# Attention, ELU block and routed experts on one core: three instruction orders around PSUM banks, and another way to spread the routing's maximum

## The chip, the cores and the metric

The kernel runs on one core of one Trainium2 chip. The metric is the device time of one execution in microseconds (us), taken as the median of several runs. The core has TensorE (PE in the profile, PEld for its weight loads), VectorE (DVE), ScalarE (ACT), GpSimd (POOL) and SyncE (SP, which here only issues DMAs). Matmuls write into the eight banks of PSUM. VectorE and ScalarE read the results from there.

## The reference, cut to what matters

Three stages follow one another. The middle one is the ELU block, the last one the routed experts:

```python
x = attention(q, k, v)                        # window of 64 keys, 4 x 8 heads, 2304 tokens in all
x = elu(x @ w_in) @ w_out                     # 512 -> 2048 -> 512
logits = x @ w_gate                           # 2304 x 8
logits = logits - logits.max()                # one maximum over the whole matrix
P = np.exp(logits)
for _ in range(8):
    P /= P.sum(1, keepdims=True) + 1e-09
    P /= P.sum(0, keepdims=True) + 1e-09
    P *= N / E
for e in range(8):
    out += P[:, e:e+1] * (np.maximum(x @ w1[e], 0.0) @ w2[e])
```

## The kernel before, in words

The order of every engine's instructions is the order in which the Python code emits them. The whole kernel stands in one manually scheduled block, and each engine, and each engine's DMA queue, works through its own list in that order. Products keep fp32 accuracy: an operand is split into a high and a low part, and three products (high by high, high by low, low by high) are added up in PSUM. So a block of 384 columns is six matmuls for a 256-row operand, and so on.

The attention comes first, then the ELU block. When the last blocks of the ELU block are done, the logits are formed, and the routing's parts (`sink_parts`, lines 625 to 697) are emitted one by one between the steps of the first experts. Part `p0` (line 629) takes the maximum of the logits along the free axis with VectorE, line 631, so that each of 128 partitions has its own maximum `mx`. Part `p1` (line 639) turns that column into a row by a product with the identity (line 641) and reduces the row to one negated number `nb` on one partition (line 643). Part `p2` (line 646) spreads that number over 128 partitions by a product with a row of ones (line 648), copies it out of PSUM (line 650) and takes the exponential on ScalarE (line 651). Then `rows` (lines 656 to 665) and `cols` (lines 667 to 674) do the eight normalizations. Each `cols` adds up the partitions by a product with ones (`csum`, line 669). Between them run the first experts in a simple form, `e_in` (lines 965 to 979, tile `p`, low part at line 260) and `e_out` (lines 981 to 999, tile `ac`, summed at line 1009). At the same time the weights for later are prepared: GpSimd makes sums of weight blocks (line 784), ScalarE their high parts (line 799) and VectorE their low parts (line 804).

The rest of the experts (from 639 us on) runs as a fast matrix scheme with seven block products in place of eight. Its loop, from line 1687 on, has a counter `s`. Seven values of `s` make one period. A period has one token group `g` of three and one quarter of an expert's hidden width. In each step there are two calls of `l1` (first product, tiles `la` and `lb`, two PSUM banks each, line 1205) and, eight steps later, one call of `l2` (second product, tiles `oa` and `ob`, line 1374 for group 0 and line 1287 in `l2_flip` for the others). `pairs` (line 1028) says which two of the seven products (`pi`) a step forms, and `out_order` (line 1033) the order of the second products. An accumulated first product is read out between its parts: `keep` copies `la` to SBUF on ScalarE (line 1225, tiles `a`, `u`, `v`), and later parts are added onto the same bank. VectorE adds such a copy to `lb` (lines 1219 and 1245), which frees that bank. The scaled form for groups 1 and 2 multiplies by the routing weights at line 1215. The high parts of the hidden values are made by ScalarE (`hid`, line 1178) and the low parts by VectorE or GpSimd (`hid_low`, lines 1183 and 1187). These wait in the list `after`, of which each call of `l1` takes up to two, and are emitted behind the call's own instructions. Some weights come raw and are split on the way: high by ScalarE (line 1113), low by GpSimd (line 1115), emitted by `w_part`.

For group 0 a second product is weighted and added to the output sum by three VectorE instructions (line 1392). In the last period of the group these write the tile `fo`, which SyncE's queue sends out (line 1397). For groups 1 and 2 the output sum stands transposed, and is added at line 1304. At the very end most of it is transposed by VectorE (line 1330) and sent by 16 DMAs, half of them issued by ScalarE's queue (line 1336). The last four 128-column blocks are transposed by TensorE in `out_unit` (line 1316) into the two `lb` banks (tile `ot`), copied out by ScalarE (line 1321; for the last block, `c == 3`, by VectorE, line 1319) and sent by SyncE's queue (line 1323).

Of the kernel before, what the change touches and what calls it, by code (L numbers as in the profile page):

```python
# [11 lines left out]
AF = mybir.ActivationFunctionType  # L12
ALU = mybir.AluOpType
AX = mybir.AxisListType
# [4 lines left out]
def kernel(  # L19
# [14 lines left out]
    nc = tc.nc  # L34
# [3 lines left out]
    E, _, FF = w1.shape  # L38
    P = 128
# [24 lines left out]
    mask = const.tile([P, P], F32, name="mask")  # L64
# [18 lines left out]
    ident = const.tile([P, P], F32, name="ident")  # L83
    ones = const.tile([P, P], F32, name="ones")
    Lg = const.tile([P, NTT, E], F32, name="Lg")
    Pr = const.tile([P, NTT, E], F32, name="Pr")
# [24 lines left out]
    def ps_sm(name):  # L111
        return ps.tile([P, 512], F32, tag="sm", bufs=1, name=name)
# [510 lines left out]
    sk = {}  # L623

    def sink_parts():
        def small(shape, nm):
            return const.tile(shape, F32, name=nm)

        def p0():
            mx = small([P, 1], "mx")  # L630
            nc.vector.tensor_reduce(mx, Lg, axis=AX.XY, op=ALU.max)
            sk["mx"] = mx
            t = work.tile([P, TB], F32, tag="m", bufs=2, name="Pe")
            Pe = t[:, :(NTT + 1) * (E + 1)].rearrange("p (t e) -> p t e", e=E + 1)
            nc.gpsimd.memset(Pe[:, :, E:], 1e-9)
            nc.gpsimd.memset(Pe[:, NTT], 1e-9 / P)
            sk["Pe"], sk["Pw"] = Pe, Pe[:, :NTT, :E]

        def p1():
            t = ps_sm("mxT")  # L640
            nc.tensor.matmul(t[0:1, :P], sk["mx"], ident, start=True, stop=True)
            nb = small([1, 1], "nb")
            nc.vector.tensor_reduce(nb, t[0:1, :P], axis=AX.X, op=ALU.max, negate=True)
            sk["nb"] = nb

        def p2():
            t = ps_sm("nbB")
            nc.tensor.matmul(t[:, 0:1], ones[0:1, :], sk["nb"], start=True, stop=True)
            nm = small([P, 1], "nm")
            nc.vector.tensor_copy(nm, t[:, 0:1])  # L650
            nc.scalar.activation(sk["Pw"], Lg, AF.Exp, bias=nm)
            sk["rs"] = small([P, NTT], "rs")
            sk["cs"] = small([P, E], "cs")
            sk["rc"] = small([P, E], "rc")

        def rows():
            rs, cs = sk["rs"], sk["cs"]
            nc.vector.tensor_reduce(rs, sk["Pe"][:, :NTT], axis=AX.X, op=ALU.add)
            nc.vector.reciprocal(rs, rs)
            nc.vector.tensor_tensor(  # L660
                out=sk["Pw"], in0=sk["Pw"], in1=rs.unsqueeze(2).to_broadcast([P, NTT, E]), op=ALU.mult
            )
            nc.vector.tensor_reduce(
                cs, sk["Pe"][:, :, :E].rearrange("p t e -> p e t"), axis=AX.X, op=ALU.add
            )

        def cols(to=None):
            t = ps_sm("csum")
            nc.tensor.matmul(t[:, :E], ones, sk["cs"], start=True, stop=True)
            rc = sk["rc"]  # L670
            nc.vector.reciprocal(rc, t[:, :E])
            nc.vector.scalar_tensor_tensor(
                sk["Pw"] if to is None else to, sk["Pw"], float(NT) / E, rc.unsqueeze(1).to_broadcast([P, NTT, E]),
                op0=ALU.mult, op1=ALU.mult,
            )

        def first():
            p2()
            rows()

        def mid():
            cols()
            rows()

        def flip():
            f = Pr.rearrange("p t e -> p (t e)")
            n = NTT * E - P
            t = ps_sm("prT")
            nc.tensor.transpose(t[:, 0:P], f[:, 0:P], ident)
            nc.tensor.transpose(t[:n, P:2 * P], f[:, P:], ident)  # L690
            st = work.tile([P, TB], F32, tag="m", bufs=2, name="prT")
            nc.scalar.activation(st[:, 0:P], t[:, 0:P], AF.Copy)
            nc.scalar.activation(st[:n, P:2 * P], t[:n, P:2 * P], AF.Copy)
            nc.sync.dma_start(out=prd[0:P], in_=st[:, 0:P])
            nc.sync.dma_start(out=prd[P:P + n], in_=st[:n, P:2 * P])

        return [p0, p1, first] + [mid] * 7 + [lambda: cols(Pr), flip]


# [470 lines left out]

    chains = {}
    H = {}
    after, late = [], []

    def hid(key, slot, src, relu):
        h = P2["hp"].tile([P, 2, TH], R32, tag=f"h{slot}", bufs=3, name=f"h{slot}")
# [15 lines left out]
    def l1(k, n, p, pi):  # L1192
# [20 lines left out]
        def scaled(t, i):  # L1213
            if g:
                nc.vector.tensor_tensor(out=t, in0=t, in1=pb[g, e][:, i], op=ALU.mult)  # L1215
# [18 lines left out]
        if pi == 1:  # L1234
            keep("a")
        elif pi == 2:
            add("c11", "a")
            put(0, "c11", True)
        elif pi == 6:
            keep("u")  # L1240
        elif pi == 5:
            keep("v")
            c = d["C"][:, :TH]
            t = tmp("c", 5, "c22")
            nc.vector.tensor_tensor(out=t, in0=c, in1=d["v"], op=ALU.add)  # L1245
            scaled(t, 1)
            d["c22"] = t
            put(2, "c22", True)
        elif pi == 3:
            d["r21"] = tmp("s", 6, "r21")  # L1250
            if g:
                nc.vector.scalar_tensor_tensor(
                    d["r21"], o, 0.0, pb[g, e][:, 1], op0=ALU.max, op1=ALU.mult
                )
            else:
                nc.scalar.activation(d["r21"], o, AF.Relu)  # L1256
            ssum("s3", "c11", "r21", ALU.subtract)
            ssum("s1", "c22", "r21", ALU.add)
            ssum("s2", "c11", "s1", ALU.subtract)
            put(5, "s3", False)  # L1260
            put(4, "s2", False)
            put(3, "s1", False)
        elif pi == 4:
            def rest():
                add("c21", "u")
                ssum("s4", "c21", "s2", ALU.add)
                put(1, "c21", True)
                put(6, "s4", False)

            late.append(rest)  # L1270
            del chains[key]
# [40 lines left out]
    def out_unit(g, acT, i, c):  # L1312
        o = P2["ps2"].tile([P, 512], F32, tag="lb", bufs=2, name="ot")
        for t in range(TH // P):
            a = i * TH + t * P
            nc.tensor.transpose(o[:, t * P:(t + 1) * P], acT[:, c, a:a + P], ident)
        st = tmp("s", 6, "ost")
        if c == 3:
            nc.vector.tensor_copy(st, o[:, :TH])
        else:  # L1320
            nc.scalar.activation(st, o[:, :TH], AF.Copy)
        t0 = (2 * g + i) * TH
        nc.sync.dma_start(
            out=out[t0:t0 + TH, c * P:(c + 1) * P].rearrange("(t p) d -> p t d", p=P),
            in_=st.rearrange("p (t d) -> p t d", d=P),
        )
# [16 lines left out]
    ot = {}  # L1343
    banks = ["oa", "ob"]

    def l2(k, x):
        g, e, pp = periods[k]
        pi = out_order[x]
        if x == 0:
# [31 lines left out]
                    )  # L1381
        if done:
            fo = P2["fin"].tile([P, 3, HB2], F32, tag=f"o{i}{j}", name="fo")
        for c in range(3):
            tt = 3 * i + c
            pe = Pr[:, g * 6 + tt, e:e + 1]
            a = oa[g][:, tt, j * HB2:(j + 1) * HB2]
            src = o[:, c * HB2:(c + 1) * HB2]
            if init and e == 0 and pp == 0:
                nc.vector.tensor_scalar(a, src, pe, None, op0=ALU.mult)  # L1390
            else:
                nc.vector.scalar_tensor_tensor(
                    fo[:, c] if done else a, src, pe, a, op0=ALU.mult, op1=ALU.add
                )
        if done:
            t0 = (2 * g + i) * TH
            nc.sync.dma_start(
                out=out[t0:t0 + TH, j * HB2:(j + 1) * HB2].rearrange("(c p) d -> p c d", p=P),
                in_=fo,
            )  # L1400


    with tc.manual_schedule():
# [280 lines left out]
        ps2_cm, P2["ps2"] = pool("ps2", space=PSUM)  # L1684
        w2_load(0)
        nw2 = 1
        for s in range(NPD * 7 + LAG):
            k, j = divmod(s, 7)
            if k < NPD:
                for z, (p, pi) in enumerate(pairs[j]):  # L1690
                    fs = after[:2]
                    del after[:2]
                    l1(k, s * 2 + z, p, pi)
                    for f in fs:
                        f()
                    w1_load(s * 2 + z + NW1)
                    w_part((1, s * 2 + z + 4))
                    if ltasks and s >= 6:
                        ltasks.pop(0)()
            if s == LAG - 3:  # L1700
                l2(0, 0)
            elif s > LAG:
                l2(*divmod(s - LAG, 7))
            for n in (0,) if s == 2 else (s - LAG + 2, s - LAG + 3):
                if s == 2 or n > 0 and (n % 7 == 0) == (n == s - LAG + 3):
                    w_part((2, n))
# [70 lines left out]
```

## Time and profile before

| what | us |
|---|---|
| median of 3 runs | 1940.57 |
| lowest and highest of them | 1939.26, 1941.41 |
| the profiled execution's own time | 1940.71 |
| its span, first to last instruction | 1938.9 |
| TensorE busy in it | 1921.7 |
| VectorE busy | 1649.8 |
| GpSimd busy | 1103.8 |
| ScalarE busy | 958.8 |

The profiled execution's own time is 1.8 us more than its span. A number in square brackets behind a row of the timeline is how long that engine had been idle before the instruction, and what it had waited for. The matmuls are pipelined: the record of one reaches over the start of the next. So what a wait costs TensorE is read from start to start.

### The profile page before, as it was taken

The numbers are of one execution on the slowest core, as the hardware profiler recorded it, in microseconds if no ns is written. First come the engines' busy times: TensorE is split into PE (matmuls) and PEld (weight loads), VectorE is DVE, ScalarE is ACT, GpSimd is POOL, SyncE is SP. The second block draws the span as 40 slices with busy tenths as digits, with TensorE's granted clock in tenths as the row PEclk, the third lists the DMA queues.
The fourth block names the chain that finished last, engine by engine and source line by source line (L and its number), as shares of the span: only waits on it lengthen the run. The fifth ranks groups of instructions, "written<-read, shape, count | busy, mean of one in ns | idle before, by whom it ended". The sixth has DMA issues, their size and how long they took to land.

```text
span 1938.9 us, 34435 instructions
## 1 busy us (share of the span) xinstructions
PE 1921.7 (99%) x11988; PEld 1812.2 (93%) x11988; DVE 1649.8 (85%) x2720; ACT 958.8 (49%) x2139; POOL 1103.8 (57%) x1081
## 2 busy tenths in 40 slices
PE   8999999999999999999999999999999999999998
PEld 6778888888888999999999999999999999999998
DVE  7867787967797799888797998998999898998997
ACT  8875545555643545554445444444344444444442
POOL 6623365756464765555455666666565566665662
PEclk9999999999999999999999999999999999999999
DMA  9851366678987688887778766766787867666665
GB/s 205 188 114 56 123 220 199 224 242 309 326 288 264 207 298 286 279 271 256 236 236 241 229 195 198 223 192 200 252 247 232 242 204 206 216 198 208 206 217 149
DMA packets 387693, 430.47 MB, mean 222 GB/s; under 512 B 113712, under 2 KB 281792, under 8 KB 384832
## 3 DMA queue, kind: packets, MB, share of 16 engines
q1 hardware_dynamic: 383136, 427.58, 71.4%
q8 instruction: 96, 1.57, 0.3%
q10 hardware_dynamic: 4384, 0.69, 0.2%
q14 instruction: 77, 0.63, 0.1%
HBM read 339.49 MB, written 84.48 MB: 219 GB/s over the span
## 4 chain that ended last, share of the span: by engine, by line
PE 87%; DVE 8%; ACT 2%; DMA 1%; issue 1%; POOL 1%; SPq 0%; DVEq 0%; ACTq 0%; POOLq 0%
PE la L1205 17%; PE lb L1205 13%; PE ob L1287 11%; PE oa L1287 11%; PE oa L1374 4%; PE ob L1374 4%; PE p L217 2%; PE p L218 2%; PE p L219 2%; PE ac L571 2%; PE ac L570 2%; PE ac L572 2%; DVE s L1229 1%; PE p L523 1%; PE p L976 1%
## 5 line engine op out<-in xcount | busy, mean ns | idle before, releaser
L1187 POOL TENSOR_TENSOR h<-s,h 128x384 fp32r<-128x384 f32 x352 | 396.8, 1145 | 408.1 <-ACT h L1178 368.8
L1205 PE MATMUL la<-xf,w1f 128*128 128x384 f32 x2112 | 416.8, 335 | 1.1 <-ACT u L1225 0.5
L1205 PEld LDWEIGHTS la<-xf,w1f 128*128 128x128 f32 x2112 | 367.4, 188 | 2.8 <-ACT u L1225 1.1
L1205 PE MATMUL lb<-xf,w1f 128*128 128x384 f32 x1584 | 317.4, 334 | 1.0 <-DVE c L1245 0.9
L1178 ACT ACTIVATE h<-s 128x384 fp32r<-128x384 f32 x352 | 179.5, 522 | 276.0 <-DVE s L1229 266.1
L1205 PEld LDWEIGHTS lb<-xf,w1f 128*128 128x128 f32 x1584 | 277.0, 188 | 2.3 <-DVE c L1245 1.9
L1115 POOL TENSOR_TENSOR w1f<-r,w1f 128x256 fp32r<-128x256 f32 x234 | 207.4, 894 | 92.6 <-ACT w1f L1113 87.1
L1178 ACT ACTIVATE h<-c 128x384 fp32r<-128x384 f32 x264 | 138.5, 525 | 237.0 <-DVE c L1215 210.9
L1287 PE MATMUL oa<-h,w2f 128*128 128x384 f32 x1344 | 251.3, 334 | 0.0
L1287 PE MATMUL ob<-h,w2f 128*128 128x384 f32 x1344 | 251.1, 334 | 0.2 <-DVE acc L1304 0.2
L1183 DVE SCALAR_TENSOR_TENSOR h<-c,h 128x384 fp32r<-128x384 f32 x264 | 217.5, 833 | 33.6 <-ACT h L1178 31.7
L1287 PEld LDWEIGHTS ob<-h,w2f 128*128 128x128 f32 x1344 | 234.5, 188 | 0.5 <-DVE acc L1304 0.5
L1287 PEld LDWEIGHTS oa<-h,w2f 128*128 128x128 f32 x1344 | 234.4, 188 | 0.1
L1215 DVE TENSOR_TENSOR c<-c,pb 128x384 f32<-128x384 f32 x192 | 177.2, 923 | 6.6
L1229 DVE SCALAR_TENSOR_TENSOR s<-c,s 128x384 f32<-128x384 f32 x176 | 124.4, 707 | 12.8 <-DVE s L1229 0.5
L1229 DVE SCALAR_TENSOR_TENSOR s<-c,r 128x384 f32<-128x384 f32 x176 | 128.7, 771 | 5.9 <-ACT r L1256 3.7
L1304 DVE TENSOR_TENSOR acc<-oa,acc 128x768 f32<-128x768 f32 (+1 forms) x114 | 104.6, 919 | 14.5 <-PE oa L1287 14.5
L1115 POOL TENSOR_TENSOR w2f<-r,w2f 128x512 fp32r<-128x512 f32 x78 | 115.8, 1499 | 0.0
L1304 DVE TENSOR_TENSOR acc<-ob,acc 128x768 f32<-128x768 f32 (+1 forms) x110 | 100.8, 919 | 13.6 <-PE ob L1287 13.6
L784 POOL TENSOR_TENSOR sw<-rw 128x256 f32<-128x256 f32 x72 | 61.9, 859 | 85.6 <-DVE g L804 67.6
L1374 PE MATMUL ob<-w2f,h 128*128 128x256 f32 x756 | 97.3, 282 | 0.2 <-DVE h L1183 0.2
L1374 PE MATMUL oa<-w2f,h 128*128 128x256 f32 x756 | 97.0, 282 | 0.0
(193 smaller groups left out, 3836.0 us busy)
## 6 DMA issues: line engine op xcount, KB each, us to landing
w2f<-wdo SPq DMA_DIRECT2D x200, 512.0 KB, 4.6
w1f<-wdi SPq DMA_DIRECT2D x382, 256.0 KB, 4.7
r<-in_moe_w_dram SPq DMA_DIRECT2D x234, 128.0 KB, 4.6
r<-in_moe_w_dram SPq DMA_DIRECT2D x108, 256.0 KB, 5.8
rw<-in_moe_w_dram SPq DMA_DIRECT2D x36, 512.0 KB, 6.0
wdi<-g SPq DMA_DIRECT2D x18, 1024.0 KB, 5.7
wdo<-g SPq DMA_DIRECT2D x18, 1024.0 KB, 5.6
qw<-in_moe_w_dram SPq DMA_DIRECT2D x28, 512.0 KB, 4.4
```

The source lines that it names most:

```text
L217: nc.tensor.matmul(p1, w1h[:, c, :], xh[:, c, :], start=(c == 0), stop=False)
L784: nc.gpsimd.tensor_tensor(out=sw[:, o], in0=a, in1=b, op=ALU.add if add else ALU.subtract)
L1115: sub.tensor_tensor(out=lo, in0=a, in1=r(hi), op=ALU.subtract)
L1178: nc.scalar.activation(h[:, 0], src, AF.Relu if relu else AF.Copy)
L1183: nc.vector.scalar_tensor_tensor(h[:, 1], src, 0.0, r(h[:, 0]), op0=ALU.max, op1=ALU.subtract)
L1187: nc.gpsimd.tensor_tensor(out=h[:, 1], in0=src, in1=r(h[:, 0]), op=ALU.subtract)
L1205: nc.tensor.matmul(o, w[:, a, c, :], x[:, b, c, :], start=first and c == 0 and z == 0, stop=last and c == 1 and z == 2, skip_group_check=True,
L1215: nc.vector.tensor_tensor(out=t, in0=t, in1=pb[g, e][:, i], op=ALU.mult)
L1229: nc.vector.scalar_tensor_tensor(d[nm], d[a], 0.0, d[b], op0=ALU.max, op1=op)
L1287: nc.tensor.matmul(o[:, c], w[:, p, b, c * P:(c + 1) * P], hs[p][:, a, :], start=fresh and p == 0 and z == 0, stop=False, skip_group_check ...
L1304: nc.vector.tensor_tensor(out=a, in0=src, in1=a, op=ALU.add)
L1374: nc.tensor.matmul(o[:, c * HB2:(c + 1) * HB2], hs[p][:, a, c * P:(c + 1) * P], w[:, p, b, :], start=fresh and c != 1 and p == 0 and z == ...
```

## The change

The change has four parts. The routing's maximum is spread in another way: `p0` multiplies the identity by the column of maxima (a diagonal matrix, written into the tile `mask`), and `p1` multiplies ones by it, so that all partitions hold the row of maxima. VectorE then reduces all 128 partitions at once, and `p2` has no product and no copy. In `l2`, the three additions of a finished block of group 0, and its DMA, are put off where the next step contains product 5, until behind the addition that frees `lb`. At step 7 the last hidden value of the second `l1` call is kept back until behind the first `l1` call of step 8. At the end, block 0 is copied out by VectorE too.

```diff
         def p0():
             mx = small([P, 1], "mx")
             nc.vector.tensor_reduce(mx, Lg, axis=AX.XY, op=ALU.max)
-            sk["mx"] = mx
+            nc.vector.tensor_scalar(mask, ident, mx, None, op0=ALU.mult)
...
         def p1():
             t = ps_sm("mxT")
-            nc.tensor.matmul(t[0:1, :P], sk["mx"], ident, start=True, stop=True)
-            nb = small([1, 1], "nb")
-            nc.vector.tensor_reduce(nb, t[0:1, :P], axis=AX.X, op=ALU.max, negate=True)
-            sk["nb"] = nb
+            nc.tensor.matmul(t[:, :P], ones, mask, start=True, stop=True)
+            sk["nm"] = small([P, 1], "nm")
+            nc.vector.tensor_reduce(sk["nm"], t[:, :P], axis=AX.X, op=ALU.max, negate=True)

         def p2():
-            t = ps_sm("nbB")
-            nc.tensor.matmul(t[:, 0:1], ones[0:1, :], sk["nb"], start=True, stop=True)
-            nm = small([P, 1], "nm")
-            nc.vector.tensor_copy(nm, t[:, 0:1])
-            nc.scalar.activation(sk["Pw"], Lg, AF.Exp, bias=nm)
+            nc.scalar.activation(sk["Pw"], Lg, AF.Exp, bias=sk["nm"])
...
-    after, late = [], []
+    after, late, behind = [], [], []
...
             nc.vector.tensor_tensor(out=t, in0=c, in1=d["v"], op=ALU.add)
+            while behind:
+                behind.pop(0)()
             scaled(t, 1)
...
-        if c == 3:
+        if c in (0, 3):
             nc.vector.tensor_copy(st, o[:, :TH])
         else:
             nc.scalar.activation(st, o[:, :TH], AF.Copy)
...
-    def l2(k, x):
+    def l2(k, x, soon):
...
+        def accumulate():
+            for c in range(3):
...
+            if done:
...
+        if done and soon:
+            behind.append(accumulate)
+        else:
+            accumulate()
...
+        held = []
         for s in range(NPD * 7 + LAG):
...
                     l1(k, s * 2 + z, p, pi)
+                    fs, held = held + fs, []
+                    if (s, z) == (7, 1):
+                        held = [fs.pop()]
                     for f in fs:
                         f()
...
-                l2(0, 0)
+                l2(0, 0, False)
             elif s > LAG:
-                l2(*divmod(s - LAG, 7))
+                l2(*divmod(s - LAG, 7), any(pi == 5 for _, pi in pairs[(s + 1) % 7]))
```

The body of `accumulate` is the loop over three blocks and the DMA that stood there before.

## Rows read from the trace of the kernel before

**Rows 1.** The page, part 1: busy time and share of each engine.

```profile
PE 1921.7 (99%) x11988; PEld 1812.2 (93%) x11988; DVE 1649.8 (85%) x2720; ACT 958.8 (49%) x2139; POOL 1103.8 (57%) x1081
```

**Rows 2.** TensorE's waits from 640 us on: total, times, longest (us).

```profile
PE lb L1205 <- DVE c L1245: 0.9, 2, 0.7
...
PE la L1205 <- POOL xf L1068: 0.4, 1, 0.4
```

**Rows 3.** Busy time of each engine in two stretches, then clock, DMA share, GB/s.

```profile
1380.00:1420.00 40.00, 39.84 (x230) 39.52 (x230) 38.44 (x54) 17.43 (x40) 24.65 (x22) 1.00 0.73 237
...
1020.00:1380.00 360.00, 360.00 (x2078) 359.80 (x2076) 321.48 (x429) 161.69 (x358) 223.81 (x206) 1.00 0.69 213
```

**Rows 4.** Timeline around the routing's maximum: start, duration, engine, line, operation, [idle before].

```profile
536.54 0.29 DVE L631 TENSOR_REDUCE mx<-Lg 128x1 f32<-128x144 f32 x1
...
536.95 1.72 POOL L784 TENSOR_TENSOR sw<-rw,sw 128x256 f32<-128x256 f32 x1
537.04 0.09 PEld L641 LDWEIGHTS mxT<-ident,mx 128*1 128x1 f32 x2 [0.35 <-DVE mx L631]
...
541.33 0.39 PE L995 MATMUL ac<-f,hl 128*128 128x512 f32 x1
...
542.58 0.50 PE L976 MATMUL p<-xh,f 128*128 128x512 f32 x1
...
545.08 0.14 DVE L650 COPY nm<-nbB 128x1 f32<-128x1 f32 x1
...
545.77 0.32 DVE L658 TENSOR_REDUCE rs<-Pe 128x18 f32<-128x162 f32 x1 [0.55 <-ACT Pe L651]
...
547.14 0.45 DVE L663 TENSOR_REDUCE cs<-Pe 128x8 f32<-128x152 f32 x1
...
548.16 0.29 PE L669 MATMUL csum<-cs,ones 128*128 128x8 f32 x2
...
582.88 0.30 PEld L669 LDWEIGHTS csum<-cs,ones 128*128 128x128 f32 x2 [0.52 <-DVE cs L663]
```

**Rows 5.** VectorE's groups by form: two copies (busy, mean ns).

```profile
L1421 DVE COPY mask<-mask 128x128 f32<-128x128 f32 x2 | 0.6, 286 | 1.5 <-POOL mask L1416 1.5
L1319 DVE COPY ost<-ot 128x384 f32<-128x384 f32 x1 | 0.6, 556 | 1.1 <-PE ot L1316 1.1
```

**Rows 6.** The page, part 5: GpSimd's weight sums (busy, mean ns).

```profile
L784 POOL TENSOR_TENSOR sw<-rw 128x256 f32<-128x256 f32 x72 | 61.9, 859 | 85.6 <-DVE g L804 67.6
```

**Rows 7.** Timeline of ScalarE, then of TensorE, around steps 7 to 9.

```profile
660.68 0.53 ACT L1178 ACTIVATE h<-s 128x384 fp32r<-128x384 f32 x1 [0.30 <-DVE s L1229]
661.11 0.40 ACT L1113 ACTIVATE w1f<-r 128x256 fp32r<-128x256 f32 x1
661.42 0.47 ACT L1225 ACTIVATE u<-la 128x384 f32<-128x384 f32 x1
...
660.22 1.21 PE L1205 MATMUL lb<-xf,w1f 128*128 128x384 f32 x6
661.94 2.58 PE L1205 MATMUL la<-xf,w1f 128*128 128x384 f32 x12 [0.51 <-ACT u L1225]
```

**Rows 8.** Timeline around a finished block of group 0.

```profile
1005.49 1.21 PE L1205 MATMUL la<-xf,w1f 128*128 128x384 f32 x6
1005.64 1.25 DVE L1392 SCALAR_TENSOR_TENSOR fo<-ob,Pr,acc 128x256 f32<-128x256 f32 x3
...
1007.41 1.31 PE L1205 MATMUL lb<-xf,w1f 128*128 128x384 f32 x6 [0.71 <-DVE c L1245]
```

**Rows 9.** Timeline of the end.

```profile
1932.58 1.02 DVE L1304 TENSOR_TENSOR acc<-oa,acc 128x384 f32<-128x384 f32 x2 [1.34 <-PE oa L1287]
1933.11 0.87 ACT L1321 ACTIVATE ost<-ot 128x384 f32<-128x384 f32 x2 [14.01 <-PE ot L1316]
...
1933.65 0.69 PEld L1316 LDWEIGHTS ot<-ident,acc 128*128 128x128 f32 x6 [1.02 <-ACT ost L1321]
```

**Rows 10.** Busy time by engine, clock, DMA share and GB/s near the end.

```profile
1934.00:1936.00 2.00, 0.59 (x5) 0.31 (x3) 0.56 (x1) 0.49 (x1) 0.00 (x0) 1.00 0.87 226
```

More of the change, by code (lines that the diff above doesn't have):

```diff
@@ L1383, in l2 @@
             fo = P2["fin"].tile([P, 3, HB2], F32, tag=f"o{i}{j}", name="fo")
[L1384 to L1393, printed above, removed]
-                )
[L1395 to L1400, printed above, removed]
+        def accumulate():
+            for c in range(3):
+                tt = 3 * i + c
+                pe = Pr[:, g * 6 + tt, e:e + 1]
+                a = oa[g][:, tt, j * HB2:(j + 1) * HB2]
+                src = o[:, c * HB2:(c + 1) * HB2]
+                if init and e == 0 and pp == 0:
+                    nc.vector.tensor_scalar(a, src, pe, None, op0=ALU.mult)
+                else:
+                    nc.vector.scalar_tensor_tensor(
+                        fo[:, c] if done else a, src, pe, a, op0=ALU.mult, op1=ALU.add
+                    )
+            if done:
+                t0 = (2 * g + i) * TH
+                nc.sync.dma_start(
+                    out=out[t0:t0 + TH, j * HB2:(j + 1) * HB2].rearrange("(c p) d -> p c d", p=P),
+                    in_=fo,
+                )
+        if done and soon:
+            behind.append(accumulate)
+        else:
+            accumulate()
     with tc.manual_schedule():
```

## The prediction

> **What bounds the kernel.** I read four views in this order. The page says that TensorE is busy 99% of the span, VectorE 85% [rows 1]. So a change has to take it from single, named waits. The list of TensorE's waits from 640 us on shows how little is left there: 0.9 us behind VectorE's addition that frees the `lb` bank, in 2 waits of which one is 0.7, and a few smaller ones [rows 2]. The windows show why: in 360 us of groups 1 and 2 TensorE never stops, VectorE is at 321 of 360 us. There is one stretch, 1380 to 1420, in which VectorE is at 38.4 of 40 us [rows 3]. The timeline then gives the places of the change. In each the question is when the next matmul starts, and when it would have started without the wait.
>
> About 0.2%, or 3.9 us of 1940.57, is what a measurement of this kernel can tell from no change.
>
> **The routing's maximum.** Before, TensorE stands in `p2` for the small product `nbB`. Its last block matmul starts at 541.33, the next one at 542.58 [rows 4]. The step from one 512-column matmul to the next is 0.23 us: in the 360 us of rows 3, 2078 matmuls of 384 columns fill TensorE, 0.173 each, and 512 columns are a third more. So `nbB` with its wait costs 542.58 - 541.33 - 0.23 = 1.02 us. The change takes this product away; nothing of `p2` is left on TensorE, and about 0.1 us of slow restart after the tiny product goes too.
>
> It adds one VectorE instruction in `p0`, 128x128 in SBUF. The trace has no such product with a column; the nearest row is a copy of the same shape, 0.29 us [rows 5]. It stands in front of `p1`'s product, for which TensorE already waits: the weight load of `mxT` stood 0.35 us until `mx` was done [rows 4]. So its whole length falls on TensorE: 0.29 us and a hand-over of some 0.03. The product itself has 128 weight columns in place of one, but `ones` can be loaded during the wait, and the 128 moving columns are as before: I take 0.05 more. The bounds of these two are 0.2 (the multiply shorter than the copy) and 1.0 us (held up, below). Net: 1.02 + 0.1 - 0.37 = **0.75 us won**, between 0.1 and 0.95.
>
> On VectorE the multiply adds 0.29. The copy out of PSUM, 0.14, goes [rows 4]. The reduction reads 128 partitions in place of one, along the same 128 elements, so I give it the same time. The exponential no longer waits for the copy of 545.08, and follows the reduction directly; so the wait of 0.55 before `rs` goes too [rows 4]. Then `cs` is ready 0.29 - 0.14 - 0.55 = -0.4 us, that is 0.4 earlier than 547.59, at 547.2. TensorE, now 0.75 earlier, comes to `csum` at 548.16 - 0.75 = 547.4. So the next thing that could be late, is not, by 0.2 us.
>
> How long the multiply is held up depends on GpSimd. From 536.95 GpSimd runs a weight sum of 1.72 us, where the mean of this group is 0.86 [rows 4, 6]: beside VectorE's two-input work such an instruction takes twice as long. The multiply has only one tensor input, as the copy of rows 5 has. The Trainium skill (SBUF — State Buffer, "Who interferes with whom") says that VectorE and GpSimd share a pair of ports as an exclusive lock, and that `tensor_scalar` in its two-port mode takes part: who issues first holds it, the other waits for the whole instruction. By this rule a multiply that comes behind GpSimd's instruction waits for its end. That is a rival below.
>
> **The held hidden value.** At step 9 the matmul into `la` waits until ScalarE has copied `u` out. TensorE's six matmuls start at 660.22, so the next was due at 660.22 + 6 x 0.173 = 661.26, and started at 661.94: 0.68 us, plus 0.1 for the slow restart. ScalarE did a hidden value at 660.68, a weight part at 661.11 and then `u` at 661.42 [rows 7]. The change puts that hidden value behind `u`. It had itself waited 0.30 for VectorE, so the weight part and `u` move up by 0.43 and that idle time, 0.73 together, and `u` is done at 661.42 + 0.47 - 0.73 = 661.16. That is before 661.26, so the wait goes: **0.8 us won** (0.5 to 1.0, the upper end since the low part of the weights also moves ahead of that value's low part on GpSimd). Queued behind the held value are only `h` for `c11`, which waits for VectorE anyway, and its own low part on GpSimd; its consumer is `l2` with product 3, five steps later. No DMA moves.
>
> **The put-off additions.** In the last period of group 0, TensorE's six `la` matmuls begin at 1005.49, so `lb` was due at 1006.53; it came at 1007.41: 0.88 us, and 0.1 of restart. VectorE did the three additions from 1005.64, 1.25 us, and then the addition that frees `lb` [rows 8]. Now that addition comes 1.25 us earlier. That is more than 0.88, so the wait goes: **0.95 us won** (0.7 to 1.0). It happens once: only group 0 comes this way, and of its four finished blocks only product 4's has product 5 in the next step. The block's bank is read one addition later, but is written again only two steps on. SP's output DMA moves behind a `w2` load and a `w1` load, which no longer queue behind it; the `w1` loads run nine calls ahead, so no one waits for them. ScalarE's `c22` value comes no later, since its scaling stood behind the additions in both orders.
>
> **The end.** ScalarE issues output DMAs until 1933 and copies blocks 0 and 1 only from 1933.11. TensorE's weight load for block 2 waits 1.02 us, until 1933.65, for block 0's bank. VectorE is idle for 1.34 us before 1932.58 [rows 9]. There the copy of block 0 fits (block 3's, of the same shape and engine, took 0.56 [rows 5]). Then block 2 waits for its own sum, the first of the two additions from 1932.58, done near 1933.1: 0.5 us earlier. But the last DMAs run through busy engines: 0.87 of 1934 to 1936 [rows 10]. Idle there are 0.13 x 2 = 0.26 us, and that is what earlier issues can use. I take 0.4 between the two (0 to 0.5). The Trainium skill (DMA: Bandwidth & Descriptors, "Issuing engines are not separate DMA queues") says that all queues end on the same 16 engines, and that issuing from another one saves only issue time. By that alone the end would give 0.26 at most, and the sum would be 0.14 smaller.
>
> **Sum.** 0.75 + 0.8 + 0.95 + 0.4 = 2.9 us, with all upper ends 3.45, with all lower ends 1.3. Against the profiled execution's own 1940.71 (its span of 1938.9 and 1.8 around it) that is 1937.8; the median of the runs, 1940.57, lies 0.14 lower, so I say **1937.7**. The waits that stay are those for GpSimd's `xf`, 0.4 [rows 2], and VectorE's around 1415: they are paced by work that hangs on TensorE's own results, so they move with it.
>
> **Rivals.**
>
> *The multiply is locked out.* GpSimd's 1.72 us instruction of rows 4 starts 0.12 us after `mx` ends. If it holds the ports, the multiply ends at 538.7 + 0.29 = 539.0 and `mxT` starts 2.0 us later than at 537.04 rather than 0.32. The sum falls by 1.65 to 1.25 us: 1939.3. For it: the doubled time. Against it: VectorE's queue has the multiply right behind `mx`, in front of that start. Chance 0.12.
>
> *The win is given back.* VectorE paces the kernel in 1380 to 1420 [rows 3]. If its backlog there does not begin earlier when TensorE does, the 2.5 us won before are lost as a longer wait at 1415, and only the end remains: 1940.2. Against it: in the 360 us before VectorE has 38 us without work, so its backlog starts anew from what TensorE hands it. Chance 0.10.
>
> *More.* The later wait for `cs` at 582.88, 0.52 us [rows 4], goes with the earlier start of the normalizations, and all terms are at their upper ends: 3.45 + 0.5 = 4.0 us, 1936.6. Against it: at 582 VectorE's order is set by the weight preparation, not by the start. Chance 0.13.
>
> *Slower.* VectorE is what truly paces the routing, so that an earlier TensorE is worth nothing there nor later, while each thing added to VectorE counts: the multiply 0.29, held up for 1.72, less the copy 0.14, gives +1.9 us: 1942.4. It decides where VectorE has no idle time between the routing and 1415. Against it speak VectorE's 85%, and its 0.55 wait for the exponential within 9 us of `mx`. Chance 0.05.
>
> *The edits do not hit their waits*: the weight part, now ahead of `u`, waits for its DMA, or the put-off block is another one. Then 1.75 us are missing: 1939.4. The part ran without a pause of its own behind the hidden value [rows 7]. Chance 0.05; the forecast has the other 0.55.
>
> **The numbers.** The forecast's own range is 1936.9 to 1938.7 (upper ends of the terms, lower ends of two, and the runs' scatter). The range for 8 in 10 takes in the lockout and missed edits up to 1939.4, and below most of the larger case: 1936.2 to 1939.6. Beyond 0.2% faster lies what is under 1936.69: the larger case and the scatter of the forecast, 0.20. Slower by over 0.2% would be over 1944.4, which none of the cases reaches; 0.04 for what I did not see. The rest, 0.76, is within 0.2%.
>
> **What would show it.** In the changed profile: no `nbB`, the multiply between `mx` and the weight parts with its length and GpSimd's beside it, `mxT` near 537.4; `u` ahead of the hidden value and no wait at `la` near 661; `lb` without its 0.7 us wait near 1005; block 0 copied by VectorE ahead of its two last additions, and block 2's weight load near 1930.6 (1933.65 less 2.5 and 0.5). The prediction is wrong if any of these waits stands again under another name, above all at `mxT`, `csum` or at 1415, or if the total moves by over 4 us.

## The result: 13 us slower, and the profile after

The changed kernel takes 1953.44 us (median of 5 runs, 1952.90 to 1954.62), the kernel before 1940.26 beside it (5 runs): a ratio of 1.0068, interval 1.0058 to 1.0079. The span is 1951.1 us, against 1938.9. I had forecast 1937.7 and a range up to 1939.6.

The page of the changed kernel, part 1 and two groups of the last stage's matmuls in part 5 (busy us, mean ns of one, then the idle time before them):

```profile
PE 1936.5 (99%) x11986; PEld 1824.2 (93%) x11986; DVE 1650.0 (85%) x2721; ACT 958.9 (49%) x2138; POOL 1103.6 (57%) x1081
...
L1200 PE MATMUL la<-xf,w1f 128*128 128x384 f32 x2112 | 422.1, 338 | 0.9 <-POOL w1f L1110 0.4
...
L1371 PE MATMUL ob<-w2f,h 128*128 128x256 f32 x756 | 97.4, 283 | 0.2 <-DVE h L1178 0.2
```

The same two groups of the kernel before:

```profile
L1205 PE MATMUL la<-xf,w1f 128*128 128x384 f32 x2112 | 416.8, 335 | 1.1 <-ACT u L1225 0.5
...
L1374 PE MATMUL ob<-w2f,h 128*128 128x256 f32 x756 | 97.3, 282 | 0.2 <-DVE h L1183 0.2
```

VectorE, ScalarE and GpSimd are as busy as before [rows 1]. TensorE is busy 14.8 us longer, with two matmuls less (those of `nbB`). So the time is not in a new wait. The list of TensorE's waits in the changed kernel from 640 us on says the same: `lb`'s 0.9 us and `u`'s wait [rows 2, 7] are gone, and nothing long has come.

```profile
PE la L1200 <- POOL w1f L1110: 0.4, 1, 0.4
PE ot L1313 <- DVE acc L1301: 0.3, 1, 0.3
PE la L1200 <- POOL xf L1063: 0.3, 1, 0.3
```

Each matmul takes longer instead. The window 1020 to 1380 of the changed kernel, with the columns of [rows 3]: TensorE never stops, as before, and the granted clock is 1.00, but it does 2052 matmuls in place of 2078. From start to start that is 360 / 2052 = 175.4 ns in place of 173.2.

```profile
1020.00:1380.00 360.00, 360.00 (x2052) 360.00 (x2051) 320.18 (x426) 161.44 (x356) 222.44 (x206) 1.00 0.67 210
```

The timeline of TensorE shows which ones. First the kernel before, from 1202.33 us on (start, duration of the merged group):

```profile
1202.33 1.20 PE L1205 MATMUL lb<-xf,w1f 128*128 128x384 f32 x6
1203.37 1.20 PE L1205 MATMUL la<-xf,w1f 128*128 128x384 f32 x6
1204.41 2.24 PE L1287 MATMUL oa<-h,w2f 128*128 128x384 f32 x12
1206.49 1.20 PE L1205 MATMUL lb<-xf,w1f 128*128 128x384 f32 x6
```

Then the changed kernel:

```profile
1202.53 1.23 PE L1200 MATMUL la<-xf,w1f 128*128 128x384 f32 x6
1203.60 1.20 PE L1200 MATMUL lb<-xf,w1f 128*128 128x384 f32 x6
1204.64 2.27 PE L1284 MATMUL ob<-h,w2f 128*128 128x384 f32 x12
1206.74 1.23 PE L1200 MATMUL lb<-xf,w1f 128*128 128x384 f32 x6
```

A round of 24 matmuls lasted 1206.49 - 1202.33 = 4.16 us, and now 1206.74 - 1202.53 = 4.21. The first six behind a change between `l1` (`xf`, `w1f`) and `l2` (`h`, `w2f`) are longer; the second group of `l1` is not. The single starts of the two traces, read out as differences in ns:

```
before, l2 after l1: 173 173 174 173 173 174 | 173 173 174 173 173 174
after,  l2 after l1: 170 174 178 185 176 181 | 174 173 174 172 174 174
after,  l1 after l2: 173 175 177 185 176 182 | 172 175 173 173 174 174
```

That is some 25 ns for each switch. Between 1169 and 1911 us there are 357 switches: 357 x 25 = 8.9 us. A matmul of the changed kernel begins 3.99 us later than its like before at 1169 us, and 12.88 later at 1911, 8.89 more.

**What could do that.** The diff has one side effect that I did not cost: the tile `nb` is no longer made. It held one number, but took 32 bytes of every partition in SBUF, at byte 4032, near the bottom of the stack of tiles that grows from the left. All tiles that stand above it on the left now begin 32 bytes lower: `w2f` at 16512 in place of 16544, `h0` at 47232 in place of 47264. The tiles stacked from the right, the lowest `w1f` (161952) and `xf0` (184480) among them, stay. Before, all of these addresses left a rest of 160 when divided by 256; now the left ones leave 128.

### The profile page after: what moved, and what is told of

Its sections match the earlier page's. It is cut to its first block, busy times and chain, and to the rows that moved or that the text cites. A ratio compares the mean times of both kernels' runs of the same rounds, so it can differ in the third digit from the quotient of the medians.

```text
span 1951.1 us, 34430 instructions
## 1 busy us (share of the span) xinstructions
PE 1936.5 (99%) x11986; PEld 1824.2 (93%) x11986; DVE 1650.0 (85%) x2721; ACT 958.9 (49%) x2138; POOL 1103.6 (57%) x1081
## 4 chain that ended last, share of the span: by engine, by line
PE 93%; DVE 2%; DMA 2%; ACT 1%; POOL 1%; SPq 1%; issue 1%; DVEq 0%; POOLq 0%; ACTq 0%
PE la L1200 19%; PE lb L1200 14%; PE ob L1284 12%; PE oa L1284 12%; PE oa L1371 5%; PE ob L1371 5%; PE ac L570 3%; PE p L218 3%; PE p L219 3%; PE p L217 3%; PE ac L571 3%; PE ac L572 3%; PE p L523 1%; PE p L971 1%; PE p L972 1%; PE p L973 1%
## 5 line engine op out<-in xcount | busy, mean ns | idle before, releaser
L1200 PE MATMUL la<-xf,w1f 128*128 128x384 f32 x2112 | 422.1, 338 | 0.9 <-POOL w1f L1110 0.4
```

The costliest lines, as they stand in the source:

```text
L1200: nc.tensor.matmul(o, w[:, a, c, :], x[:, b, c, :], start=first and c == 0 and z == 0, stop=last and c == 1 and z == 2, skip_group_check=True,
```

## The experiments

The theory: where TensorE's operands stand in SBUF, relative to one another, sets the spacing behind a switch. The rival: one of the four edits slows TensorE by its order or its instructions.

### Give back the 32 bytes, or take them from the kernel before

`e1_after_fill32` is the changed kernel with an unused tile of the same size:

```diff
             t = ps_sm("mxT")
+            small([1, 1], "nb")
             nc.tensor.matmul(t[:, :P], ones, mask, start=True, stop=True)
```

> The changed kernel with one unused 32-byte column kept where nb was, so that every SBUF address is that of the kernel before. Placement theory: the change's loss comes from the tile nb that it no longer makes, which moves every later tile of that side of SBUF by 32 bytes; then the 384-column matmuls of the second half go back from 175.4 to 173.4 ns from start to start, and the time falls to about 1937.7 us (the sum of the prediction). Order theory: one of the four new orders slows TensorE itself; then it stays at 1953 us.

`e2_before_less32` is the kernel before, with `nb` as a second column of `nm`, so that one tile less is made:

```diff
-            nb = small([1, 1], "nb")
+            sk["nm2"] = small([P, 2], "nm")
+            nb = sk["nm2"][0:1, 1:2]
...
-            nm = small([P, 1], "nm")
+            nm = sk["nm2"][:, 0:1]
```

> The kernel before with nb put into a second column of the tile nm, so that its later tiles move by 32 bytes as in the changed kernel, and with no other change. Placement theory: it becomes as slow as the changed kernel or a little slower, 1953 to 1956 us, with 175.4 ns from matmul to matmul. Order theory: it stays at 1940 us.

The medians, in us (the changed kernel's is that of the first section, beside 1940.26; the others are beside the 1939.99):

| | left tiles at the old place | left tiles 32 bytes lower |
|---|---|---|
| order of before | 1939.99 | 1954.55 (ratio 1.0076, 1.0063 to 1.0090) |
| order of the change | 1938.37 (ratio 0.9990, 0.9981 to 0.9998) | 1953.44 (ratio 1.0068) |

The window 1020 to 1380 of `e1_after_fill32`:

```profile
1020.00:1380.00 360.00, 360.00 (x2079) 360.00 (x2078) 322.94 (x431) 161.34 (x356) 224.35 (x206) 1.00 0.68 215
```

and of `e2_before_less32`:

```profile
1020.00:1380.00 360.00, 360.00 (x2052) 360.00 (x2051) 319.39 (x424) 161.37 (x357) 222.98 (x206) 1.00 0.65 210
```

The matmuls are 2079 and 2052: they go with the place and not with the order. At the end of the traces the placement costs 14.3 us in either order (2.07 earlier to 12.26 later, and 0 to 14.31 later), in the medians 15.1 and 14.6. The edits save 2.07 and 2.05 us at the end of the traces, 1.6 and 1.1 in the medians. That the pairs from the traces agree so closely is luck: at 205 us, ahead of every edit, traces of kernels with the old spacing already lie between 1.4 us earlier and 0.8 later than that of before. The rival falls: the four edits are a gain of 0.1%, which is within the 0.2% of the prediction, and the loss is the tile. Set beside the trace of `e1_after_fill32`, that of the changed kernel loses 8.9 us between 1169 and 1911 us, 3.3 between 639 and 1169, 0.8 in the first experts from 493 us on, and 2.1 ahead of them, part of it this scatter; at the very end it is 0.9 us shorter.

### Is it the place itself, or the distance?

`e3_after_right32` moves the right tiles down by 32 bytes too, with a longer unused tile at the right edge (line 69):

```diff
-    pad.tile([P, 416], F32, name="pad")
+    pad.tile([P, 424], F32, name="pad")
```

> The changed kernel with the pad tile at the other end of SBUF 32 bytes longer, so that the tiles stacked from that end move by 32 bytes too: both sides at 0 of 64 bytes, where the kernel before has both at 32 of 64. If a mixture of the two is what is slow, about 1938 us; if 0 of 64 is slow as such, 1953 us or more. Order theory: 1953 us.

It takes 1937.48 us, ratio 0.9987 (0.9978 to 0.9997), the lowest median of several runs here. Its window:

```profile
1020.00:1380.00 360.00, 360.00 (x2079) 360.00 (x2078) 323.02 (x431) 161.63 (x357) 224.48 (x206) 1.00 0.68 216
```

The left tiles stand where they stood in the slow kernel and the right ones 32 bytes off their old place, and the spacing is the old one. So it is not the new address of the left tiles that is slow, but their place relative to the right ones. `e4_after_nogap` leaves out the unused `gap` tile of line 65, which brings the left tiles 64 bytes below their old place:

> The changed kernel without its unused 32-byte tile gap, so that the tiles of the first side move by 32 bytes more, 64 from the kernel before, back to 32 of 64; the small constants (ones, identity, logits) come to 0 of 64. If the place within 64 bytes counts, about 1938 us. If what counts is the distance from the old place, or the exact addresses, it stays slow, 1948 us or more. Order theory: 1953 us.

It takes 1952.69 us, ratio 1.0065 (1.0051 to 1.0079), with the same pattern of 171 175 177 185 176 182 behind a switch:

```profile
1020.00:1380.00 360.00, 360.00 (x2053) 360.00 (x2052) 320.04 (x426) 161.44 (x356) 222.69 (x206) 1.00 0.67 209
```

So 64 bytes off are as bad as 32; the loss doesn't grow from one to the other.

### How far must it be?

Four kernels shorten the `pad` tile, so that the right tiles move up by 96, 224, 480 and 992 bytes, and with the left ones 32 lower the distance is 128, 256, 512 and 1024 bytes more than before. The edit is that of line 69, with 392, 360, 296 and 168 in place of 416.

> The changed kernel (first side 32 bytes down) with the pad at the other end 96 bytes shorter, so that the two sides come 128 bytes nearer than in the kernel before. If the places count within 128 bytes: fast, about 1938 us. If within a longer stretch, or if only the old distance is fast: slow, about 1951 us, like the 32 and 64 bytes.

> The change, and the tiles stacked from the right begin 224 bytes higher; left ones stay 32 lower than before: the distance between w1f and w2f is 256 bytes more than in the kernel before (142 times 1024 there). If the distance must be a multiple of 1024 bytes, the second layers' 384-column matmuls stand about 175.4 ns apart and the time is near 1953 us. If a multiple of 256 will do, 173.4 ns and near 1938 us. If only one exact distance is good, near 1953 us.

> The change, and the tiles stacked from the right begin 480 bytes higher: the distance between w1f and w2f is 512 bytes more than in the kernel before. If it must be a multiple of 1024: about 175.4 ns from one 384-column matmul to the next and near 1953 us; if a multiple of 512 or of 256 will do: 173.4 ns and near 1938 us; if only one exact distance is good: near 1953 us.

> The change, and the tiles stacked from the right begin 992 bytes higher: the distance between w1f and w2f is 1024 bytes more than in the kernel before. If the distance counts by a period of 1024 bytes or of a part of it: 173.4 ns and near 1938 us. If only one exact distance is good: 175.4 ns and near 1953 us.

One run each: 1944.48, 1938.36, 1938.65 and 1936.93 us (the kernel before beside them 1941.29 for the first and 1939.44 for the others). A single time says little, since 21 runs of the kernel before lie between 1937.37 and 1943.41 us; the spacing in the trace says more. The window of `e9_right_up224`:

```profile
1020.00:1380.00 360.00, 360.00 (x2079) 360.00 (x2078) 322.87 (x431) 161.62 (x357) 224.46 (x207) 1.00 0.69 215
```

and of `e8_right_up96`:

```profile
1020.00:1380.00 360.00, 360.00 (x2075) 359.83 (x2074) 322.33 (x431) 162.49 (x360) 223.98 (x207) 1.00 0.68 213
```

256, 512 and 1024 bytes more are as good as none (2079 matmuls in the window for all three). Of the distances tried, those that change by a multiple of 256 are fast. With 128 the last stage is nearly fast (174 174 175 behind a switch, then 173), but the one time is still 1944.48. Set beside the trace of `e9_right_up224`, it loses 2.1 us between 205 and 380 us, 0.7 between 493 and 536, and 2.6 from 639 to 1911. The first of these is in the ELU block. Half of its eight buffers of each weight tile (`w0h`, `w0l`, `w1h`, `w1l`) are stacked from the left and half from the right. The mean time from one 512-column matmul to the next, in ns, read out from the traces by stretches:

```
us              205-260  260-320  320-380  380-440  440-490
before            226.7    227.5    226.7    227.7    226.7
after             226.7    230.1    233.3    228.3    226.7
e3_after_right32  226.7    227.6    226.8    227.5    226.7
e8_right_up96     226.7    229.6    232.4    228.5    226.7
e9_right_up224    226.7    227.5    226.7    227.7    226.7
```

From 205 to 260 and from 440 to 490 us the changed kernel has the old spacing to a tenth: a stage whose operands keep their places to one another loses nothing. In between it loses up to 6.6 ns per matmul. The order of the kernel says what differs. The ELU block has four parts of the hidden width, and they use the two halves of the weight buffers in turn (line 182, `wslot[u % 2]`; the first half is opened with `side="right"`, the second from the left). The parts `u = 1` (some 203 to 293 us in the changed kernel) and `u = 3` (400 to 506) read weights on the left, `u = 2` (302 to 394) weights on the right. The moving operands `xh`, `xl`, `gh` and `gl` always stand on the left. A window inside `u = 2` and one inside `u = 3`, first before, then after:

```profile
305.00:365.00 60.00, 60.00 (x266) 49.68 (x265) 52.53 (x63) 33.66 (x52) 39.80 (x39) 1.00 0.65 208
425.00:485.00 60.00, 60.00 (x270) 49.84 (x269) 46.44 (x55) 31.23 (x48) 38.19 (x45) 1.00 0.91 318
```

```profile
305.00:365.00 60.00, 60.00 (x259) 48.33 (x258) 51.97 (x62) 33.40 (x52) 37.61 (x38) 1.00 0.66 202
425.00:485.00 60.00, 60.00 (x270) 49.85 (x269) 45.71 (x53) 32.58 (x49) 39.49 (x46) 1.00 0.93 322
```

Of the two windows only that inside `u = 2` holds fewer matmuls than before. Within it all weights come from the right, so there is no change of sides between its matmuls: at 512 columns it is the place of the weights against the moving operand that costs, in every matmul (233.3 ns on average), and not a switch. So 128 bytes cost little behind the switches at 384 columns, but nearly as much as 32 at 512.

### Whose tile is it?

`e5_fill_tp`, `e6_fill_hp` and `e7_fill_w2p` are `e1_after_fill32` with unused tiles in one pool of the last stage. The first moves only tiles that VectorE, ScalarE and GpSimd use (`tp`: `c`, `a`, `s`, `u`, `v` and what lies above); the second moves `h` and those by 32 bytes; the third moves `w2f` by 32 and `h` by 1024.

```diff
+        fill = {'tp': 8}
...
+            if nm in fill:
+                P2[nm].tile([P, fill[nm]], F32, tag="fill", name="fill")
```

In place of `{'tp': 8}` the others have `{'hp': 8}` and `{'w2p': 8, 'hp': 248}`.

> The filled version of the changed kernel (every address as before), with 32 unused bytes at the front of the pool of temporaries in the last stage: only the tiles that VectorE, ScalarE and GpSimd read and write there (c, a, s, u, v, pb) move by 32 bytes, TensorE's operands stay. If the loss hangs on TensorE's own operands, the time stays at about 1938 us and the matmuls of the last stage at 173.4 ns; if it comes from other engines' accesses beside TensorE's, the last stage goes to 175.4 ns and the time to about 1949 us.

> The same with the 32 bytes at the front of the pool of hidden values h instead, so that TensorE's moving operand of the second product in groups 1 and 2 (and the stationary one in group 0) lies 32 bytes off w1f, xf and w2f. If a moving operand's place against the one before it counts: 6 slow matmuls after each switch between l1 and l2 as in the changed kernel, 175.4 ns on the mean, about 1949 us. If only the weights' places count: 1938 us.

> The same with 32 bytes at the front of the pool of w2f and 992 at the front of the pool of h (so h moves by 1024 in all): only w2f, the stationary operand of the second product in groups 1 and 2, lies 32 bytes off. If the stationary operand's place counts, the slow matmuls come back in groups 1 and 2; if only the moving one's, then they stay away there, and come in group 0, where w2f is the moving operand, if at all.

One run each: 1937.11, 1939.29 and 1941.46 us, the kernel before 1941.29. Moving the other engines' tiles changes nothing: the spacing is 173.2 ns (2078 matmuls in the window), so a clash with what they read and write there is not the cause. Moving `h` costs a little (2076 matmuls): only two matmuls behind a switch from `l2` to `l1` are longer, 175 and 179. Moving `w2f` gives half of the loss in the window 1020 to 1380 (2066 matmuls, between 2079 and 2052). The timeline of `e7_fill_w2p`:

```profile
1203.21 1.22 PE L1201 MATMUL lb<-xf,w1f 128*128 128x384 f32 x6
1204.27 1.20 PE L1201 MATMUL la<-xf,w1f 128*128 128x384 f32 x6
1205.31 2.25 PE L1285 MATMUL ob<-h,w2f 128*128 128x384 f32 x12
1207.40 1.22 PE L1201 MATMUL la<-xf,w1f 128*128 128x384 f32 x6
```

The first `l1` group is long (1.06 to the next start), `l2` is not: 12 matmuls in 2.09 us. The single differences are 178 for the last of `l2`, then 185 175 182 and 173 again: one switch of the two in a round costs some 25 ns, the other nothing. So behind the switches the weights (`w2f` against `w1f`) weigh more than the moving operand, and both directions are slow only when `h` and `w2f` are moved together. In both kernels the rests of the weights and of the moving operand of `l2` are 32 bytes apart. In the ELU block that cost every matmul of 512 columns; within `l2`, at 384 columns, it costs nothing. In group 0, where `l2` has 256 columns and `w2f` moves, `e7_fill_w2p` is even faster: its matmuls follow one another in 117 ns in place of 119, and 118 in `e6_fill_hp`. That gain is part of its 1941.46. Which pair of operands decides in each direction is left open.

### What the end's edit is worth

`e12_no_end` is `e1_after_fill32` with ScalarE's copy of block 0 back:

```diff
-        if c in (0, 3):
+        if c == 3:
```

> As e1_after_fill32, but block 0 of the last transposed output is copied by ScalarE again. If the end's edit is worth nothing because the output DMAs wait in SyncE's queue behind the eight that end at 1931.03 us, then from the first transpose into ot to the end of the span it is the same within 0.2 us. If the edit is worth the 0.4 us of the prediction, it is 0.4 us longer.

One run: 1937.19 us. From the first transpose into `ot` to the end of the span it takes 7.85 us, as the kernel before (7.85). With the edit, in the six kernels of the same spacing, it is 8.08, 7.70, 7.71, 7.39, 7.38 and 7.43: a mean of 7.62, 0.2 us less, with a scatter of more than that. The other traces widen it: `e2_before_less32`, also without the edit, has 8.16, and the changed kernel 7.19. Over all traces the mean is 7.95 without the edit (three) and 7.57 with it (eleven). So the gain is between 0.2 and 0.4 us, and these traces do not settle it.

## Why the prediction was wrong

**The step that failed** is in the first part of the sum, "The routing's maximum". There I counted what the change takes away as instructions alone: "nothing of `p2` is left on TensorE". The tile `nb`, which `p1` made, went too, and I put its going at nothing without a reason. It costs 14.3 us, five times the sum: not as a wait, but as a longer time from one matmul to the next. None of my cases had it: the rival on the slower side was VectorE's pace at +1.9 us, and of what lies beyond 1944.4 I said that none of the cases reaches it. The 0.04 "for what I did not see" was all that stood for it. The profile of before did not show the price, since all tiles stood well. The diff showed the cause: it makes one tile less in a pool above which all other tiles of the left side are stacked.

**The terms, read with the placement undone.** With the old placement the kernel takes 1938.37 us, and with both sides moved 1937.48; I had said 1937.7. That these totals come so near is in part luck, since single terms were off, and the runs of one kernel lie up to 6 us apart. Here are the rows of `e1_after_fill32` for each. (It comes to the early experts, at 493 us, 0.80 us earlier than the one trace of before. The change has no edit ahead of that point, so I leave this out of the terms.)

*The routing: 0.4 in place of 0.75.* The timeline:

```profile
535.76 0.28 DVE L631 TENSOR_REDUCE mx<-Lg 128x1 f32<-128x144 f32 x1
...
536.08 0.29 DVE L632 TENSOR_SCALAR mask<-ident,mx 128x128 f32<-128x128 f32 x1
536.16 0.79 POOL L780 TENSOR_TENSOR sw<-rw,sw 128x256 f32<-128x256 f32 x1
...
536.41 0.30 PEld L641 LDWEIGHTS mxT<-mask,ones 128*128 128x128 f32 x2 [0.53 <-DVE mask L632]
...
541.37 0.28 DVE L644 TENSOR_REDUCE nm<-mxT 128x1 f32<-128x128 f32 x1
...
541.57 1.66 DVE L800 TENSOR_TENSOR f<-rw,f 128x1024 fp32r<-128x1024 f32 x1
...
546.31 0.42 DVE L659 TENSOR_REDUCE cs<-Pe 128x8 f32<-128x152 f32 x1
...
546.79 0.39 PE L665 MATMUL csum<-cs,ones 128*128 128x8 f32 x2 [0.35 <-DVE cs L659]
```

The multiply took the 0.29 of the copy [rows 5], and the reduction of 128 partitions the time of one, 0.28. Both were as costed. The lockout rival is not met: the multiply began 0.08 us ahead of GpSimd's instruction, which took 0.79, no longer than its group's mean [rows 6]. By the Trainium skill (SBUF — State Buffer, "Who interferes with whom") the first of the two to issue holds the ports and the other waits for the whole instruction. The first was not held up here, as it says; but GpSimd's instructions just before took 0.73 and 0.74, so its 0.79 has no room for the 0.21 us that the multiply had left, and the row does not show that the second waited. Read from start to start on TensorE, the going of `nbB` gives 1.16 us (1.12 in the sum), and the new product for the maximum costs 0.10, where the sum had 0.37, although `ones` was not loaded during the wait: its load stood until `mask` was done. What failed is the sentence that `csum` is not late "by 0.2 us": its row shows a wait of 0.35, and from start to start it gives back 0.58 us, which the sum had at nothing. VectorE's chain from `mx` to the end of `cs` is 10.97 us (546.31 + 0.42 - 535.76) and was 11.05 (547.14 + 0.45 - 536.54, [rows 4]): 0.08 shorter, where I had 0.4. The wait for the exponential is gone, but VectorE's four low parts between them take longer, 6.39 us in place of 6.02. So in this stretch VectorE does pace TensorE, as the rival on the slower side said, though not at its price. From the first of the early experts (493 us) to the first fast product (639 us) the gain is 0.41, and 0.38 to 0.44 in the other traces of the changed order with the old spacing. The later wait before `csum`, which one rival let go, stayed: 0.55 at 581.67 against 0.52.

*The held value: 0.7 of 0.8.* The timeline:

```profile
659.39 0.47 ACT L1221 ACTIVATE u<-la 128x384 f32<-128x384 f32 x1
659.76 0.51 ACT L1174 ACTIVATE h<-s 128x384 fp32r<-128x384 f32 x1
...
660.06 2.29 PE L1201 MATMUL la<-xf,w1f 128*128 128x384 f32 x12
```

`u` stands ahead of the hidden value, and `la` goes without the wait of [rows 7]. Over 639 to 683 us the gain is 0.69.

*The put-off additions: 0.95, as costed.* The timeline:

```profile
1004.49 0.54 DVE L1241 TENSOR_TENSOR c<-lb,v 128x384 f32<-128x384 f32 x1
1004.95 1.25 DVE L1391 SCALAR_TENSOR_TENSOR fo<-ob,Pr,acc 128x256 f32<-128x256 f32 x3
...
1005.40 1.20 PE L1201 MATMUL lb<-xf,w1f 128*128 128x384 f32 x6
```

The wait of 0.71 [rows 8] is gone; from 692 to 1140 us the gain is 0.97 in `e12_no_end` and 0.92 in `e5_fill_tp` and `e11_right_up992`. In `e1_after_fill32` it is 0.41, since another wait takes the rest, for GpSimd's low part of a `w1f` at 692 us:

```profile
692.04 0.96 PE L1201 MATMUL la<-xf,w1f 128*128 128x384 f32 x4 [0.47 <-POOL w1f L1111]
```

It stands in the traces of the changed kernel, of `e1_after_fill32`, `e3_after_right32` and `e10_right_up480`, and not in those of `e5_fill_tp`, `e9_right_up224`, `e11_right_up992` and `e12_no_end`, which have the old spacing too. `e12_no_end` has the same instructions up to there, so it is not the change's; what sets it off from run to run I did not settle.

*The end: 0.2 to 0.4, where I had 0.4.* The timeline:

```profile
1929.30 0.56 DVE L1317 COPY ost<-ot 128x384 f32<-128x384 f32 x1 [0.35 <-PE ot L1314]
...
1930.90 0.55 PE L1314 MATMUL ot<-ident,acc 128*128 128x128 f32 x3 [0.32 <-DVE acc L1302]
...
1931.24 2.25 SPq L1321 DMA_DIRECT2D out_dram<-ost  x4
```

VectorE copied block 0 in time, and block 2's product came at 1930.90; I had said near 1930.6. But block 0's DMA is issued only at 1931.24, 1.4 us behind the end of its copy, because SyncE's queue is still issuing the transposed output, three DMAs from 1929.62 on that take 1.41 us. My 0.4 and the estimate of 0.26, which stood beside the Trainium skill (DMA: Bandwidth & Descriptors, "Issuing engines are not separate DMA queues"), both lie within what the traces leave open.

Together 0.4 + 0.7 + 0.95 + 0.2 = 2.25 us, or up to 0.2 more by the end, where I had 2.9; from 493 us to the end, the trace of `e1_after_fill32` gains 2.07 - 0.80 = 1.27 us on that of before (with the wait at 692 and the longest of the six ends), that of `e12_no_end` 3.52 - 1.48 = 2.04 (without the end's edit). "The win is given back" is not met: between 1169 and 1911 us nothing is lost.

## What to carry to other kernels

Removing or adding a tile moves every tile stacked above it, even if it holds one number: read the addresses of TensorE's operands as part of the diff. In the kernels here that kept the old spacing in the last stage, the operands of TensorE all left the same rest by 256 bytes; it is a place to begin, not a rule, since 256 columns ran a little faster with the two operands 32 bytes apart. If the page shows TensorE busy for longer with the same matmuls at the same clock, and no new waits, look at start-to-start times around changes of operands before you look at the edits; a spare tile of the lost size tells the two apart in one run.

## What was not expected of the hardware

At 384 columns the 32 bytes cost some 25 ns behind each change of operands, over six matmuls, and nothing within a run of the same ones. At 512 columns they cost 6.6 ns in each matmul (233.3 in place of 226.7) as long as weights and moving operand stand apart by them. The 256-column matmuls of the changed kernel, both of whose operands moved together, show almost none of it (group 0's second products take 283 ns on average, before 282). A distance of 128 bytes nearly spares the switches at 384 columns, but costs 5.7 ns at 512. The Trainium skill (SBUF — State Buffer, "Who interferes with whom") lists two independent read ports for TensorE and says that only the pair of VectorE and GpSimd causes contention. Read as a rule that nothing else slows a reader, it does not hold here: by it the kernels of this study should all have had one spacing in a stage, and they have 173.2 and 175.4 ns in the last one. In the ELU block the place of the weights against the moving operand raises the spacing from 226.7 to 233.3 ns, so in this sense the two reads are not independent. What TensorE does in those six matmuls no run shows.
